# A reordered front with a third quad's scores moved into it and zero matmuls in its gaps, in a fused attention and MLP kernel

## The chip, the cores and the metric

The kernel runs on one core of a Trainium2 chip. The metric is device time in microseconds (us), the median of several executions.

The engines are named as the profile names them: PE is the matmul engine, PEld its weight load, DVE is VectorE, ACT is ScalarE, POOL is GpSimd, SP is SyncE.

## The reference

```python
# q, k, v: [8, 8, 576, 64]; f: [8, 8, 576]; w_in: [512, 2048]; w_out: [2048, 512]; all float32
scores = q @ k.T / sqrt(64)
cum    = cumsum(log(clip(f, 1e-4, 1)))
scores = where(causal, scores + cum[:, None] - cum[None, :], -1e9)
attn   = softmax(scores) @ v
x      = attn, heads side by side: [4608, 512]
out    = gelu_tanh(x @ w_in) @ w_out          # [4608, 512] float32
```

The 64 pairs of batch and head are worked on in 16 "quads" of four heads; two quads make one batch. The decay is folded into v: `vw` is v times a weight per key, so that only the exponential of the scores is needed. The MLP goes in nine chunks of 512 tokens: 64 matmuls "MLP-in", 64 matmuls "MLP-out" of 128x128 weights and 512 columns each.

## The kernel before

The program order of each engine is the order in which the code emits instructions (the schedule is manual). So a function's place in the code is its place in the queue of its engine, and an instruction that waits holds up everything behind it on that engine (in the kernel before GpSimd waits 10.74 us for v, up to 15.55, and the masks that stand behind that wait start at 16.97, though ACT had written the first exponentials by 11.8).

```python
    rounds = [(0, 512), (512, 512), (1024, 512)]        # a quad's scores, in three rounds
    # ...
    psS = ctx.enter_context(tc.tile_pool(name="psS", bufs=2, space=bass.MemoryType.PSUM))
    psO = ctx.enter_context(tc.tile_pool(name="psO", bufs=1, space=bass.MemoryType.PSUM))
    psM = ctx.enter_context(tc.tile_pool(name="psM", bufs=2, space=bass.MemoryType.PSUM))
    # ...
    def load_one(src, dst, i):
        b, h0 = i // QPB, 4 * (i % QPB)
        return nc.gpsimd.dma_start(
            out=dst[i % 2].rearrange("p a d -> p (a d)"),
            in_=src[b, h0:h0 + 4].rearrange("h (p a) d -> (h p) (a d)", p=32))
    # ... transpose_words: one VectorE transpose of k (or q) into kT (or qT)
    def make_vw(i, eng):
        h0 = 4 * (i % QPB)
        vb = v_nat[(i // QPB) % 2]
        eng.tensor_mul(
            vw[i % 2][:, 0:NT], vb[:, :, h0:h0 + 4, :],
            wT[:, i, :, :].unsqueeze(3).to_broadcast([128, NT, 4, D]))

    def copy_low(i):
        nc.vector.tensor_copy(vw[i % 2][64:128, LOW], vw[i % 2][0:64, 0])
    # ...
    def score_round(i, r, by_tile):
        off, n = rounds[r]
        tiles = [psS.tile([128, 2, 512], FP32, name="ps_s", tag="s") for _ in range(2)]
        qq, p = qT[i % 2], pt[i % 2]
        parts = []
        for (key, col, q0, nq) in pieces:
            a, z = max(col, off), min(col + nq, off + n)
            if a < z:
                parts.append((key, a - off, q0 + a - col, z - a))
        for heads in ((0, 1), (2, 3)) if by_tile else (range(4),):
            for c in range(2):
                for j, (key, c0, q0, nq) in enumerate(parts):
                    for h in heads:
                        nc.tensor.matmul(
                            tiles[h // 2][:, h % 2, c0:c0 + nq],
                            key_columns(i, key, h, c),
                            qq[32 * h:32 * h + 32, q0:q0 + nq, c],
                            start=(c == 0 and j == 0), stop=(c == 1),
                            skip_group_check=True,
                        )
        for g in range(2):
            nc.scalar.activation(p[:, 2 * g:2 * g + 2, off:off + n], tiles[g], AF.Exp, scale=scale)
    # ... mask(i, r): GpSimd affine_select on the diagonal blocks of that round
    # ... product(i, groups, spare): 24 matmuls into po (psO), or into a psS tile if spare
    def denominators(i):

        def column(h):

            return lambda t: (w_bf[:, i, t, h:h + 1] if t not in (0, LOW) else
                              w_bf[:, i, t, h:h + 1].to_broadcast([128, 32]))

        po = product(i, [(32 * h, column(h), h) for h in range(4)], False)
        den = den_pool.tile([128, S], FP32, name="den", tag="den")
        nc.vector.transpose(out=den, in_=po)
        rec = den_pool.tile([128, S // 32], FP32, name="rec", tag="rec")
        nc.vector.reciprocal(rec, den[:, 0:S:32])
        rb = den_pool.tile([128, S], FP32, name="rb", tag="rb")
        nc.vector.transpose(out=rb.rearrange("p (c j) -> p c j", j=32),
                            in_=rec.unsqueeze(2).to_broadcast([128, S // 32, 32]))
        rbs[i] = rb

    def attn_out(i, x, spare=False):
        b, u = i // QPB, i % QPB
        po = product(i, [(32 * h, lambda t, h=h: vw[i % 2][:, t, h, x:D:2], h) for h in range(4)], spare)
        nc.vector.tensor_mul(xT[:, 2 * u + x, S * b:S * (b + 1)], po, rbs[i])
    # ... mlp_in(c, pairs): 8 matmuls per pair into a psS tile, GELU on ScalarE
    # ... mlp_out(c): generator, one matmul of 64 per step; fill = mlp_out(c)
    def setup():
        nc.sync.dma_start(out=f_sb, in_=f.rearrange("b h s -> (b h) s"))
        k0 = load_qk(0)[0]
        # ... masks
        load_qk(1)
        v0 = load_v(0, 0, 4)
        after(v0[0], k0)
        v0 += load_v(0, 4, 4)
        w_in_dmas.append(load_w_in(0))
        after(w_in_dmas[0], v0[7])
        w_in_dmas.append(load_w_in(1))
        # ... memsets on VectorE, log of f, transposes of quad 0
    def step(i, j, fill, fills, extra=(None, None, None)):

        first = i is not None and i < 2
        for r in range(3):
            if i is not None:
                score_round(i, r, first)
                if i == 0 and r == 0:
                    make_w()
            if j is not None:
                if r == 0:
                    denominators(j)
                else:
                    attn_out(j, r - 1, spare=(i is None and r == 1))
            if i is not None:
                if i == 0 and r == 0:
                    transpose_k(1)
                    transpose_q(1)
                if r == 0 and first:
                    make_vw(i, nc.vector)
                    copy_low(i)
                mask(i, r)
                if r == 1 and not first:
                    make_vw(i, nc.gpsimd)
                if r == 2 and not first:
                    copy_low(i)
            if extra[r]:
                extra[r]()
            pull(fill, fills[r])
    # prepare(*quads): transpose_k, transpose_q of each, then load_qk(i + 2)
    with tc.manual_schedule():
        setup()
        step(0, None, none, (0, 0, 0),
             (None, None, lambda: w_in_dmas.extend(load_w_in(c) for c in (2, 3))))
        w_out_dmas = []
        step(1, 0, none, (0, 0, 0),
             (lambda: load_qk(2),
              lambda: w_out_dmas.extend(load_w_out(c) for c in (0, 1)),
              lambda: w_out_dmas.extend(load_w_out(c) for c in (2, 3))))
        load_qk(3)
        v1 = load_v(1)
        after(v1[0], w_out_dmas[2])
        step(None, 1, none, (0, 0, 0))
        fill = none
        for c in range(NCH):

            mlp_in(c, (0, 1))
            for x in fill:
                pass
            if c == 0:
                prepare(2, 3)
                load_v(2)
            elif c + 1 < B:
                prepare(2 * c + 3, 2 * c + 4)
                if c + 2 < B:
                    load_v(c + 2)
            for pr in range(2, NP):
                mlp_in(c, (pr,))
            fill = mlp_out(c)
            if c == 0:
                pull(fill, 6)
                step(2, None, fill, (9, 8, 7))
                prepare(4)
                step(3, 2, fill, (6, 6, 5))
                step(4, 3, fill, (5, 5, 4))
            elif c + 1 < B:
                i = 2 * c + 3
                pull(fill, 6)
                step(i, i - 1, fill, (12, 8, 8))
                step(i + 1 if i + 1 < NQ else None, i, fill, (8, 7, 7))
```

One PSUM tile `po` (`psO`, one buffer) takes the products of a quad one after another: the denominators, then two value products; each must be read by DVE before the next may start. And after the first two quads, PE fills every wait of the attention with matmuls of the MLP-out (`pull(fill, n)`); before the first MLP-in there is nothing to fill with.

The softmax here doesn't subtract the row's maximum and nothing guards it: scores larger than these inputs give would overflow.

## Time and profile before

| | before |
|---|---|
| time | 354.88 us (354.87 to 354.94) |
| span of the profiled run | 353.4 us |
| first MLP-in matmul | 32.17 us |
| first MLP-in to second MLP-in | 43.09 us |
| second to third | 35.67 us, then 36.56 each |

From the page of the profile before: the span, and the granted clock of PE in 40 slices of 8.8 us, in tenths of full rate.

```profile
span 353.4 us, 7265 instructions
...
PEclk9866999999999999999999999999999999999999
```

As far as it is recorded, the clock is low in the second to fourth slices only. The record begins at 12.34 us; that PE ran at half clock before that is read from its matmuls (a score matmul of 448 columns takes 0.56 us at 8.7, as it does at 16.2 where the record says 0.50, and 0.36 at 12.4 where it says 1.0). The windows view of before, cut at the stages; its columns are the stretch, its length, the busy time of PE, PEld, DVE, ACT and POOL (with counts), the granted clock, the share of DMA and GB/s:

```profile
0.00:32.17 32.17, 19.08 (x265) 9.57 (x267) 18.85 (x40) 16.51 (x18) 17.67 (x34) 0.80 0.92 170
32.17:46.93 14.76, 14.03 (x62) 6.27 (x63) 4.71 (x5) 7.05 (x7) 1.58 (x3) 0.98 1.18 202
46.93:75.26 28.33, 25.30 (x370) 11.43 (x373) 11.98 (x18) 19.36 (x20) 15.38 (x19) 1.00 0.75 158
75.26:110.93 35.67, 34.95 (x373) 16.04 (x379) 14.81 (x22) 22.84 (x24) 13.49 (x18) 1.00 0.42 97
```

In the front PE is busy 19 of 32 us; in the stretch of the first MLP-out 25.3 of 28.3; after that it is nearly full, 34.95 of 35.67. The PE timeline of before (start, length, engine, line, operation, out<-in, form, count, and in brackets the idle time before it with what ended it). L215 is the product with the attention weights, L255 is MLP-in:

```profile
27.64 1.53 PE L215 MATMUL po<-pt,w_bf 128*32 128x512 bf16 x24 [0.85 <-DVE xT L244]
...
30.30 1.53 PE L215 MATMUL po<-pt,vw 128*32 128x512 bf16 x24
32.17 3.73 PE L255 MATMUL ps_h<-xT,w_in_sb 128*128 128x512 bf16 x15 [0.33 <-issue]
...
62.60 0.87 PE L215 MATMUL po<-pt,vw 128*32 128x512 bf16 x24 [0.20 <-DVE den L233]
```

A product of 24 matmuls takes 1.5 us at half clock and 0.87 us at full clock. From the view of waits of before (who waited for what: total, times, longest), GpSimd stood behind a late load:

```profile
POOL w_in_sb L120 <- DMA v_nat<-in_v_dram: 10.7, 1, 10.7
```

From the chain of waits of before (start, length, what), the stretch that sets the date of the first value product of quad 2 at 62.60:

```profile
49.99 6.43 DMA v_nat<-in_v_dram
56.59 2.34 POOL vw L154
58.95 0.64 DVE vw L159
```

v of the second batch comes late, since its load waits for w_out.

### The profile page before, as it was taken

The page shows a single profiled execution, that of the slowest core. Times are in us where ns is not written, and L with a number is a line of the kernel's source. Part 1 is how long each engine was busy: PE and PEld are TensorE (multiplying, and loading weights), DVE is VectorE, ACT ScalarE, POOL GpSimd, SP SyncE. Part 2 cuts the span into 40 slices and gives each one's busy share as a digit, 9 for nine tenths or more (in the row PEclk, how much of TensorE's full clock was granted, in tenths as well). Part 3 has the DMA queues.
Part 4 walks back from the last instruction along what each step waited for, and adds up shares of the span by engine and source line. Part 5 has one row for each costly group of instructions (what it writes and reads, how often), then busy time and mean ns, then how long its engine had stood idle before and what let it go on. Part 6 is the DMA issues. An engine that isn't in the chain of part 4 may idle for free.

```text
span 353.4 us, 7265 instructions
## 1 busy us (share of the span) xinstructions
PE 327.9 (93%) x3156; PEld 150.8 (43%) x3209; DVE 128.1 (36%) x188; ACT 188.6 (53%) x188; POOL 103.9 (29%) x142
## 2 busy tenths in 40 slices
PE   1778988999999999999999999999999999999995
PEld 0334433444444444444444444444444444444442
DVE  6557024635343524352355044414530360002011
ACT  3770666675756566556664667457556633520510
POOL 4294015652154205520551055204420320000000
PEclk9866999999999999999999999999999999999999
DMA  7799999507710671059113911280110011001011
GB/s 140 154 201 192 203 231 209 100 31 167 155 40 30 145 154 63 30 117 182 55 38 87 202 42 62 63 169 32 53 40 0 32 40 51 0 32 64 25 54 66
DMA packets 50688, 33.13 MB, mean 94 GB/s; under 512 B 38816, under 2 KB 40864, under 8 KB 50656
## 3 DMA queue, kind: packets, MB, share of 16 engines
q0 software_dynamic: 7808, 13.63, 22.2%
q1 hardware_dynamic: 42848, 19.03, 20.2%
q8 instruction: 25, 0.41, 0.5%
q14 instruction: 7, 0.06, 0.0%
HBM read 36.85 MB, written 9.44 MB: 131 GB/s over the span
## 4 chain that ended last, share of the span: by engine, by line
PE 77%; DMA 8%; POOL 5%; SPq 4%; issue 2%; DVE 1%; another core or an unknown queue 1%; ACT 0%; POOLq 0%
PE ps_h L255 31%; PE pso L269 31%; PE po L215 8%; PE ps_s L179 6%; SPq L108 4%; DMA w_out_sb<-in_moe_w_out_dram 4%; DMA v_nat<-in_v_dram 3%; POOL pt L193 2%; POOL vw L154 1%; DMA k_c<-in_k_dram 1%; POOL w_in_sb L120 1%; POOL w_out_sb L124 0%; DVE kT L138 0%; DVE qT L138 0%
## 5 line engine op out<-in xcount | busy, mean ns | idle before, releaser
L269 PE MATMUL pso<-w_out_sb,gT 128*128 128x512 bf16 x534 | 128.7, 379 | 4.4 <-issue 3.3
L255 PE MATMUL ps_h<-xT,w_in_sb 128*128 128x512 bf16 x565 | 126.7, 380 | 1.6 <-ACT gT L262 0.7
L262 ACT ACTIVATE gT<-ps_h 128x1024 bf16<-128x1024 f32 x72 | 72.7, 1023 | 92.4 <-PE ps_h L255 81.7
L187 ACT ACTIVATE pt<-ps_s 128x1024 bf16<-128x1024 f32 x96 | 92.8, 1021 | 45.2 <-PE ps_s L179 32.3
L255 PEld LDWEIGHTS <-w_in_sb 128*128 128x128 bf16 x576 | 56.4, 98 | 69.3 <-issue 2.2
L193 POOL TENSOR_SCALAR_AFFINE_SELECT pt<-pt 128x512 bf16<-128x512 bf16 (+2 forms) x80 | 47.3, 600 | 113.9 <-ACT pt L187 112.6
L269 PEld LDWEIGHTS <-gT 128*128 128x128 bf16 x576 | 52.6, 98 | 62.6 <-issue 0.7
L273 DVE COPY o_st<-pso 128x512 f32<-128x512 f32 x36 | 24.8, 689 | 91.1 <-PE pso L269 87.9
L179 PE MATMUL ps_s<-qT,kT 32*128 32x64 bf16 (+3 forms) x896 | 36.2, 269 | 6.4 <-ACT pt L187 3.0
L244 DVE TENSOR_TENSOR xT<-po,rb 128x576 bf16<-128x576 f32 x30 | 22.7, 757 | 37.5 <-PE po L215 37.3
L233 DVE STREAM_TRANSPOSE den<-po 128x576 f32<-128x576 f32 x16 | 12.5, 781 | 63.2 <-PE po L215 63.2
L154 POOL TENSOR_TENSOR vw<-v_nat,wT 128x1280 bf16<-128x1280 f32 x14 | 32.6, 2327 | 0.8 <-DMA v_nat<-in_v_dram 0.8
L179 PEld LDWEIGHTS <-kT 32*128 32x128 bf16 x896 | 16.5, 94 | 31.5 <-issue 25.4
L215 PE MATMUL po<-pt,vw 128*32 128x512 bf16 (+1 forms) x720 | 27.4, 289 | 1.4 <-DVE xT L244 1.2
L129 POOL DMA_DIRECT2D k_c<-in_k_dram x16 | 9.4, 586 | 48.2 <-DVE kT L138 47.4
L138 DVE STREAM_TRANSPOSE kT<-k_c 128x576 f32<-128x576 f32 x16 | 19.9, 1247 | 9.9 <-DMA k_c<-in_k_dram 9.7
L215 PEld LDWEIGHTS <-vw 128*32 128x32 bf16 x768 | 16.3, 101 | 16.6 <-issue 9.6
L138 DVE STREAM_TRANSPOSE qT<-q_c 128x576 f32<-128x576 f32 x16 | 19.8, 1237 | 0.3 <-DMA q_c<-in_q_dram 0.3
L215 PE MATMUL po<-pt,w_bf 128*32 128x64 bf16 (+5 forms) x384 | 16.3, 295 | 2.4 <-POOL pt L193 1.4
L187 ACT ACT_TABLE_LOAD x8 | 10.3, 1283 | 6.8 <-PE ps_s L179 6.8
L237 DVE STREAM_TRANSPOSE rb<-rec 128x576 f32<-128x576 f32 x16 | 12.5, 778 | 0.5
L215 PEld LDWEIGHTS <-w_bf 128*1 128x1 bf16 (+1 forms) x384 | 7.3, 89 | 12.3 <-issue 6.3
(42 smaller groups left out, 56.7 us busy)
## 6 DMA issues: line engine op xcount, KB each, us to landing
out_dram<-o_st SPq DMA_DIRECT2D x36, 256.0 KB, 2.0
v_nat<-in_v_dram SPq DMA_DIRECT2D x28, 256.0 KB, 7.5
k_c<-in_k_dram POOLq DMA_DIRECT2D x16, 288.0 KB, 6.3
q_c<-in_q_dram POOLq DMA_DIRECT2D x16, 288.0 KB, 7.6
w_in_sb<-in_moe_w_in_dram POOLq DMA_DIRECT2D x4, 512.0 KB, 7.0
w_out_sb<-in_moe_w_out_dram POOLq DMA_DIRECT2D x4, 512.0 KB, 13.0
v_nat<-in_v_dram SPq DMA_DIRECT2D x15, 128.0 KB, 5.9
f_sb<-in_f_dram SPq DMA_DIRECT2D x1, 144.0 KB, 2.9
```

Source lines behind the costliest of these rows:

```text
L108: ins.append(nc.sync.dma_start(out=v_nat[b % 2][:n, t, h0:h0 + nh, :], in_=v[b, h0:h0 + nh, 128 * t:128 * t + n, :].rearrange("h p d -> p ...
L138: nc.vector.transpose(out=dst.rearrange("p s c -> p (s c)").bitcast(FP32) .rearrange("p (t a) -> p a t", a=S // 32), in_=src.rearrange("p ...
L154: eng.tensor_mul(vw[i % 2][:, 0:NT], vb[:, :, h0:h0 + 4, :], wT[:, i, :, :].unsqueeze(3).to_broadcast([128, NT, 4, D]))
L179: nc.tensor.matmul(tiles[h // 2][:, h % 2, c0:c0 + nq], key_columns(i, key, h, c), qq[32 * h:32 * h + 32, q0:q0 + nq, c], start=(c == 0 an ...
L187: nc.scalar.activation(p[:, 2 * g:2 * g + 2, off:off + n], tiles[g], AF.Exp, scale=scale)
L193: nc.gpsimd.affine_select(out=x, in_=x, compare_op=ALU.is_ge, fill=0.0, base=0, pattern=pattern, channel_multiplier=-1)
L215: nc.tensor.matmul(po[r0:r0 + w.shape[-1], 448 + q0:448 + q0 + nq], w, p[:, h, col:col + nq], start=(key in (0, "low")), stop=(key in ("lo ...
L244: nc.vector.tensor_mul(xT[:, 2 * u + x, S * b:S * (b + 1)], po, rbs[i])
L255: nc.tensor.matmul(ph[:, j, :], w_in_sb[:, dt, 128 * ft:128 * ft + 128], xT[:, dt, CH * c:CH * (c + 1)], start=(dt == 0), stop=(dt == N_DT ...
L262: nc.scalar.activation(gT[c % 2][:, 2 * pr:2 * pr + 2, :], ph, AF.Gelu_apprx_tanh)
L269: nc.tensor.matmul(pso, gT[c % 2][:, ft, 128 * n:128 * n + 128], w_out_sb[:, ft, :], start=(ft == 0), stop=(ft == N_FT - 1))
L273: nc.vector.tensor_copy(st, pso)
```

## The change

The intent: bring loads and work into the order in which data arrive. GpSimd shall not wait for a load ahead of other work; quad 2 is scored already in the front; zero matmuls ("fillers") are to keep PE's clock up where PE would idle; some masks become DVE multiplies by a triangle; quads 3 and 4 stay beside the first MLP-out, in a new order. The core of the diff, with cuts marked by [...]:

```diff
-    def load_one(src, dst, i):
+    def load_one(src, dst, i, a0=0, na=S // 32):
         b, h0 = i // QPB, 4 * (i % QPB)
+        s = slice(D * a0, D * (a0 + na))
         return nc.gpsimd.dma_start(
-            out=dst[i % 2].rearrange("p a d -> p (a d)"),
-            in_=src[b, h0:h0 + 4].rearrange("h (p a) d -> (h p) (a d)", p=32))
+            out=dst[i % 2].rearrange("p a d -> p (a d)")[:, s],
+            in_=src[b, h0:h0 + 4].rearrange("h (p a) d -> (h p) (a d)", p=32)[:, s])
 
     def load_qk(i):
         return [load_one(k, k_c, i), load_one(q, q_c, i)]
 
[...]
-    def score_round(i, r, by_tile):
+    idle_ps = []
+
+    def keep_busy(n, cols=512):
+
+        for _ in range(n):
+            nc.tensor.matmul(idle_ps[0][:, 0:cols], idle[:, 0:128], idle[:, 0:cols],
+                             start=True, stop=True)
+
+    def score_round(i, r, by_tile=None):
[...]
+            if by_tile and r + heads[0] > 0:
+                keep_busy(*by_tile)
[...]
+    def mask_by_product(i, r, keys=("low", 0, 1, 2, 3)):
+        p = pt[i % 2]
+        for (key, col, q0, nq) in pieces:
+            if key in keys and q0 == 128 * (0 if key == "low" else key) and \
+                    rounds[r][0] <= col < rounds[r][0] + 512:
+                m = causal[1 if key == "low" else 0]
+                nc.vector.tensor_mul(p[:, :, col:col + 128], p[:, :, col:col + 128],
+                                     m.unsqueeze(1).to_broadcast([128, 4, 128]))
 
[...]
-        k0 = load_qk(0)[0]
+        k0 = [load_one(src, dst, 0, a0, S // 64) for (src, dst) in ((k, k_c), (q, q_c))
+              for a0 in (0, S // 64)][1]
[...]
-        v0 += load_v(0, 4, 4)
-        w_in_dmas.append(load_w_in(0))
-        after(w_in_dmas[0], v0[7])
-        w_in_dmas.append(load_w_in(1))
-
+        load_v(0, 4, 4)
+        for t_ in v_nat:
+            nc.gpsimd.memset(t_[64:128, HIGH, :, :], 0.0)
+        for t_ in vw:
+            nc.gpsimd.memset(t_[0:64, LOW, :, :], 0.0)
+        nc.gpsimd.memset(w_bf[0:64, :, LOW, :], 0.0)
+
+        nc.vector.memset(idle, 0.0)
[... the memsets leave VectorE; nine zero matmuls before, twelve after the transposes of log f ...]
+        for a0 in (0, S // 64):
+            transpose_k(0, a0, S // 64)
+        for a0 in (0, S // 64):
+            transpose_q(0, a0, S // 64)
 
[... step() keeps the later quads only ...]
+    def first_quads():
+        score_round(0, 0, (1, 256))
+        make_w()
+        transpose_k(1)
+        mask(0, 0)
+        load_qk(2)
+        make_vw(0, nc.gpsimd)
+        w_in = [load_w_in(c) for c in range(2)]
+        nc.vector.tensor_copy(w_bf[:, :, 0:NT, :], wT)
+        nc.vector.tensor_copy(w_bf[64:128, :, LOW, :], wT[0:64, :, 0, :])
+        transpose_q(1)
+        for r in (1, 2):
+            score_round(0, r, (2, 384))
+            mask_by_product(0, r)
+        copy_low(0)
+        transpose_k(2)
+        transpose_q(2)
+
+        score_round(1, 0, (2, 384))
+        mask(1, 0)
+        w_in.append(load_w_in(2))
+        make_vw(1, nc.gpsimd)
+        score_round(1, 1, (2, 256))
+        denominators(0, lambda: mask_by_product(1, 1))
+        score_round(1, 2, (1, 256))
+        mask_by_product(1, 2, (2,))
+        mask(1, 2, (3,))
+        w_in.append(load_w_in(3))
+        load_qk(3)
+        attn_out(0, 0)
+        attn_out(0, 1)
+        copy_low(1)
+
+        score_round(2, 0, (1, 256))
+        denominators(1)
+        score_round(2, 1, (1, 256))
+        w_out = [load_w_out(c) for c in range(4)]
+        attn_out(1, 0)
+        attn_out(1, 1)
+        score_round(2, 2, (1, 256))
+        for r in range(3):
+            mask(2, r)
+        v1 = load_v(1, 0, 4)
+        after(v1[0], w_out[1])
+        load_v(1, 4, 4)
+        return v1
+
+    def second_quads(fill, v1):
+
+        transpose_k(3)
+        transpose_q(3)
+        for r in range(3):
+            score_round(3, r)
+            mask(3, r)
+            pull(fill, 7 - (r > 0))
+        after(load_qk(4)[0], v1[-1])
+        make_vw(2, nc.gpsimd)
+        make_vw(3, nc.gpsimd)
+        denominators(2)
+        copy_low(2)
+        pull(fill, 6)
+        attn_out(2, 0, True)
+        pull(fill, 6)
+        attn_out(2, 1)
+        transpose_k(4)
+        transpose_q(4)
+        load_qk(5)
+        pull(fill, 6)
+        for r in range(3):
+            score_round(4, r)
+            if r == 0:
+                denominators(3)
+                copy_low(3)
+            else:
+                attn_out(3, r - 1)
+            mask(4, r)
+            pull(fill, 7)
+        load_qk(6)
 
[...]
-        step(0, None, none, (0, 0, 0),
-             (None, None, lambda: w_in_dmas.extend(load_w_in(c) for c in (2, 3))))
-        w_out_dmas = []
-        step(1, 0, none, (0, 0, 0),
-             (lambda: load_qk(2),
-              lambda: w_out_dmas.extend(load_w_out(c) for c in (0, 1)),
-              lambda: w_out_dmas.extend(load_w_out(c) for c in (2, 3))))
-        load_qk(3)
-        v1 = load_v(1)
-        after(v1[0], w_out_dmas[2])
-        step(None, 1, none, (0, 0, 0))
+        v1 = first_quads()
         fill = none
         for c in range(NCH):
 
             mlp_in(c, (0, 1))
             for x in fill:
                 pass
-            if c == 0:
-                prepare(2, 3)
+            if c > 0 and c + 1 < B:
+                prepare(2 * c + 3, 2 * c + 4)
+            if c == 1:
                 load_v(2)
-            elif c + 1 < B:
-                prepare(2 * c + 3, 2 * c + 4)
-                if c + 2 < B:
-                    load_v(c + 2)
+            if c > 0 and c + 2 < B:
+                load_v(c + 2)
+            if c == 1:
+                make_vw(4, nc.gpsimd)
[...]
-                step(2, None, fill, (9, 8, 7))
-                prepare(4)
-                step(3, 2, fill, (6, 6, 5))
-                step(4, 3, fill, (5, 5, 4))
+                second_quads(fill, v1)
```

## The prediction

> **What bounds the kernel now.** The span is 353.4 us, PE busy 93% (page). From about 76 us it is a steady PE-bound loop: the chain of waits repeats every 36.57 us per MLP chunk, against 128 matmuls x 0.2156 us plus two quads of about 4.2 us = 36.0. The diff hardly touches it; the slack lies before 76 us. (a) First MLP-in matmul at 32.17 us (PE timeline), with two quads, about 8.4 us of full-clock work, done. (b) From the end of the first MLP-in (46.93) to the equivalent end of the first MLP-out (about 76.0) PE needs about 24.4 us (64 matmuls 13.8, nine score rounds 5.6, six products 5.0) and takes 29.1. There the chain goes w_out, v (landed 56.4), GpSimd's vw (2.33), DVE's copy and k/q transposes, quad 2's first product at 62.6.
>
> **Front, costed.** Removed: GpSimd's 10.7 us wait for v ahead of w_in and masks (wait view). So quad 2's k/q are issued near 13 instead of 22.8 and, at the observed 4.5 us latency and 1.5 us per load, land near 18 and 19.4. But DVE now transposes them (2.4 us) before quad 0's denominators, whose transposition starts near 20.3 (before: 20.79). From there runs the same serial chain through the single po buffer: product on PE (0.8 to 1.5), DVE pass 0.76, six times, mask multiplies and score rounds between. I get quad 1's last product near 30.6 and quad 2's last exps at 32.3 and 33.2, which free the PSUM tiles for MLP-in: start 32.3 to 33.5 us. The front is not shorter; its gain is quad 2's three rounds already scored (1.9 us of PE).
>
> **Zero matmuls.** Before, the granted clock averages 0.79, 0.67, 0.86 in the stretches 10-20, 20-30, 30-40 us. [...] The fillers (21 of 512 columns, then about 6900 columns) should warm the first scores, but ACT and DVE pace this front: under 1 us.
>
> **First MLP-out.** Quad 3's exps end about 10.8 us after MLP-in's end, as quad 2's did (46.93 to 57.7). GpSimd then does two masks (1.3), issues k4/q4 (1.1), and only then vw of quad 2 (2.33), then DVE's copy: quad 2's first product again near 62.8 to 64, a PE stall of about 4 us. Second new stall: k4/q4 transposes (2.4 us) stand on DVE behind quad 2's last multiply, with six matmuls (1.3 us) to cover: about 1.8 us. These eat the three rounds saved. End of first MLP-out: 76 before, 76 to 79 after.
>
> **Predicted: 355.0 us, 8-in-10 range 349.5 to 359.5.** Faster by over 2%: 0.14; within 2%: 0.79; slower by over 2%: 0.07. The sum is +1 to +3 us; I shade it down because the filler counts look tuned on a chip.
>
> **What would show it.** Right: MLP-in starts at 32 to 34 us; DVE's first den transposition near 20 follows a wait on q_c; a 3 to 4 us PE wait ended by vw/copy near 62 and one of about 2 us at quad 4's first scores, ended by DVE's qT; period still 36.6; clock 1.0 at 6 to 20 us.
>
> **What would make it wrong.** MLP-in starting near 28 (q2 landing by 16) would move everything 4 to 5 us earlier: near 349. Half clock through the whole product chain, or late w_in, would make it slower.

That the fillers would speed up the first scores, and "under 1 us" for it, were my estimates; measured later, the clock stood at 1.0 from 5.93 us in the change and, as read from the matmuls, at one half up to 12.34 in the kernel before.

## The result, and the profile after

The changed kernel took 371.28 us (369.77 to 372.77, four runs) against 354.91 of the kernel before (354.87 to 355.99): slower, ratio 1.0454, 95% interval 1.0404 to 1.0503. Ratios here are the mean time of one kernel's fast runs over that of the other's of the same rounds, so not quite the ratio of the medians quoted. The profiled run took 369.77.

From the page of the profile after:

```profile
span 368.1 us, 7422 instructions
...
PEclk9995899879999999999999999999999999999999
```

The windows view after, at the same stages, and then two windows of 3.41 us, the step of the recorded clock (in every trace here its changes lie a multiple of 3.41 us apart):

```profile
0.00:38.05 38.05, 33.04 (x364) 14.59 (x365) 25.19 (x48) 20.60 (x22) 23.33 (x41) 0.85 1.02 181
38.05:53.69 15.64, 14.96 (x66) 6.47 (x65) 0.53 (x1) 9.37 (x9) 1.22 (x2) 0.94 0.78 142
53.69:89.07 35.38, 26.97 (x322) 11.01 (x320) 13.84 (x17) 14.12 (x15) 11.53 (x15) 0.90 0.28 58
89.07:125.87 36.80, 35.25 (x378) 15.74 (x376) 14.96 (x21) 22.28 (x23) 15.90 (x20) 1.00 0.67 142
...
23.00:26.41 3.41, 1.56 (x37) 0.90 (x36) 2.44 (x5) 0.00 (x0) 3.41 (x6) 1.00 1.13 209
26.41:29.83 3.42, 3.42 (x44) 1.39 (x45) 1.22 (x3) 2.05 (x2) 2.92 (x5) 0.50 1.07 182
```

The span grew by 14.7 us (368.1 - 353.4). The first MLP-in starts 5.88 us later; from there to the second MLP-in it takes 51.02 us (15.64 + 35.38) instead of 43.09, which is 7.93 more; from the second to the third 36.80 instead of 35.67, 1.13 more. After that the chunks take 36.56 us in both, and the end is 0.3 us shorter. Of the 7.93 and the 1.13, 0.65 us only change place: the kernel before does the last three MLP-out matmuls after the second MLP-in has begun.

The clock stands at 1.0 from 5.93 to 26.41 us, thanks to the fillers (in x5 below, without those in the score rounds, it falls at 17.2), then at one half until 40.07, and again at one half from 70.79 to 77.61. The last two lines above are the windows on either side of the first fall: in the one up to 26.41 PE was busy 1.56 of 3.41 us.

The PE timeline after (L237 is the product, L174 a filler, L192 scores, L278 MLP-in, L292 MLP-out):

```profile
21.77 0.87 PE L237 MATMUL po<-pt,vw 128*32 128x512 bf16 x24 [0.35 <-DVE den L255]
24.85 0.87 PE L237 MATMUL po<-pt,vw 128*32 128x512 bf16 x24 [2.21 <-DVE xT L267]
...
27.57 1.53 PE L237 MATMUL po<-pt,w_bf 128*32 128x512 bf16 x24
...
34.01 1.53 PE L237 MATMUL po<-pt,vw 128*32 128x512 bf16 x24 [0.87 <-DVE xT L267]
...
38.05 4.61 PE L278 MATMUL ps_h<-xT,w_in_sb 128*128 128x512 bf16 x16
...
69.16 0.40 PE L237 MATMUL ps_o<-pt,vw 128*32 128x512 bf16 x4 [3.12 <-POOL vw L157]
71.53 1.10 PE L237 MATMUL ps_o<-pt,vw 128*32 128x64 bf16 x20 [1.97 <-DVE vw L162]
...
79.88 0.69 PE L192 MATMUL ps_s<-qT,kT 32*128 32x64 bf16 x24 [1.28 <-DVE qT L141]
```

Four idle stretches of PE stand out: 2.21 us ahead of quad 0's second value product, after which the clock falls; 3.12 and 1.97 us at quad 2's first value product; 1.28 us at quad 4's scores. What ended them is in the timelines of GpSimd and DVE. GpSimd after:

```profile
20.53 2.33 POOL L157 TENSOR_TENSOR vw<-v_nat,wT 128x1280 bf16<-128x1280 f32 x1 [0.29 <-DMA v_nat<-in_v_dram]
...
23.59 0.76 POOL L122 DMA_DIRECT2D w_in_sb<-in_moe_w_in_dram  x1
...
66.74 4.64 POOL L157 TENSOR_TENSOR vw<-v_nat,wT 128x1280 bf16<-128x1280 f32 x2
```

DVE after:

```profile
20.98 0.74 DVE L255 STREAM_TRANSPOSE den<-po 128x576 f32<-128x576 f32 x1
...
21.94 1.20 DVE L223 TENSOR_TENSOR pt<-pt,causal 128x512 bf16<-128x512 bf16 x1
...
23.76 0.38 DVE L223 TENSOR_TENSOR pt<-pt,causal 128x512 bf16<-128x512 bf16 x1
...
69.14 2.34 DVE L162 COPY vw<-vw 64x256 bf16<-64x256 bf16 x1 [2.55 <-POOL vw L157]
```

A mask multiply takes 1.20 us and, two instructions later, one of the same shape takes 0.38. The slow one runs while GpSimd multiplies vw (20.53 to 22.86) and ends at 23.14, 0.28 us after it; the quick one runs while GpSimd only issues a load of w_in. The copy takes 2.34 us and ends at 71.48; GpSimd's two vw multiplies of 66.74 to 71.38 end just before. My hypothesis from these numbers: a mask multiply or a copy on DVE that begins while GpSimd multiplies vw ends only after that multiply. The experiments test it. The order of arrival matters: quad 0's first mask multiply began at 14.56, just after a vw multiply (14.39), and took 2.44 us; in x2 and x4 below it began just before that multiply and took 0.42 and 0.43. There it cost nothing further on: the third of these multiplies ends at 17.67 here and at 17.61 and 17.75 there.

### The profile page after: what moved, and what is told of

Read it like the earlier page. It is cut to its first block, busy times and chain, and to the rows that moved or that the text cites. A ratio compares the mean times of both kernels' runs of the same rounds, so it can differ in the third digit from the quotient of the medians.

```text
span 368.1 us, 7422 instructions
## 1 busy us (share of the span) xinstructions
PE 348.6 (95%) x3252; PEld 155.3 (42%) x3252; DVE 132.3 (36%) x192; ACT 189.2 (51%) x188; POOL 107.8 (29%) x146
## 4 chain that ended last, share of the span: by engine, by line
PE 70%; SPq 3%; POOL 3%; DVE 3%; DMA 2%; issue 2%; ACT 0%; POOLq 0%
PE pso L292 31%; PE ps_h L278 26%; PE po L237 8%; PE ps_s L192 5%; SPq L110 3%; POOL vw L157 2%; DMA v_nat<-in_v_dram 2%; DVE vw L162 1%; POOL pt L206 1%; PE ps_o L237 1%; DVE o_st L296 0%; DVE kT L141 0%; DVE qT L141 0%; ACT pt L200 0%; DVE den L255 0%
## 5 line engine op out<-in xcount | busy, mean ns | idle before, releaser
L292 PE MATMUL pso<-w_out_sb,gT 128*128 128x512 bf16 x576 | 136.3, 383 | 0.0
L278 PE MATMUL ps_h<-xT,w_in_sb 128*128 128x512 bf16 x576 | 128.1, 381 | 1.4 <-ACT gT L285 1.4
L206 POOL TENSOR_SCALAR_AFFINE_SELECT pt<-pt 128x512 bf16<-128x512 bf16 (+2 forms) x75 | 44.0, 594 | 144.4 <-ACT pt L200 138.8
L278 PEld LDWEIGHTS <-w_in_sb 128*128 128x128 bf16 x576 | 56.4, 98 | 70.6 <-issue 3.7
L292 PEld LDWEIGHTS <-gT 128*128 128x128 bf16 x576 | 53.0, 98 | 63.7 <-issue 2.7
L192 PE MATMUL ps_s<-qT,kT 32*128 32x64 bf16 (+3 forms) x896 | 39.8, 267 | 3.5 <-ACT pt L200 1.9
L157 POOL TENSOR_TENSOR vw<-v_nat,wT 128x1280 bf16<-128x1280 f32 x16 | 37.2, 2330 | 9.4 <-DMA v_nat<-in_v_dram 9.4
L237 PE MATMUL po<-pt,vw 128*32 128x512 bf16 (+1 forms) x720 | 28.3, 293 | 4.4 <-DVE xT L267 3.1
L192 PEld LDWEIGHTS <-kT 32*128 32x128 bf16 x896 | 17.3, 94 | 29.7 <-issue 22.5
L237 PEld LDWEIGHTS <-vw 128*32 128x32 bf16 x768 | 16.3, 101 | 26.6 <-issue 12.6
L141 DVE STREAM_TRANSPOSE kT<-k_c 128x576 f32<-128x576 f32 (+1 forms) x17 | 19.9, 1181 | 4.3 <-DMA k_c<-in_k_dram 4.3
L141 DVE STREAM_TRANSPOSE qT<-q_c 128x576 f32<-128x576 f32 (+1 forms) x17 | 19.8, 1174 | 0.8 <-DMA q_c<-in_q_dram 0.7
L237 PE MATMUL po<-pt,w_bf 128*32 128x64 bf16 (+5 forms) x384 | 14.7, 288 | 0.1
L174 PE MATMUL idle_ps<-idle 128*128 128x512 bf16 (+2 forms) x43 | 12.8, 404 | 1.3 <-DVE idle L318 1.3
(47 smaller groups left out, 72.3 us busy)
```

What stands on the lines that cost most here:

```text
L141: nc.vector.transpose(out=dst.rearrange("p s c -> p (s c)").bitcast(FP32) .rearrange("p (t a) -> p a t", a=S // 32)[:, a0:a0 + na], in_=sr ...
L157: eng.tensor_mul(vw[i % 2][:, 0:NT], vb[:, :, h0:h0 + 4, :], wT[:, i, :, :].unsqueeze(3).to_broadcast([128, NT, 4, D]))
L174: nc.tensor.matmul(idle_ps[0][:, 0:cols], idle[:, 0:128], idle[:, 0:cols], start=True, stop=True)
L192: nc.tensor.matmul(tiles[h // 2][:, h % 2, c0:c0 + nq], key_columns(i, key, h, c), qq[32 * h:32 * h + 32, q0:q0 + nq, c], start=(c == 0 an ...
L206: nc.gpsimd.affine_select(out=x, in_=x, compare_op=ALU.is_ge, fill=0.0, base=0, pattern=pattern, channel_multiplier=-1)
L237: nc.tensor.matmul(po[r0:r0 + w.shape[-1], 448 + q0:448 + q0 + nq], w, p[:, h, col:col + nq], start=(key in (0, "low")), stop=(key in ("lo ...
```

## The experiments

Theory: the front loses because a DVE mask multiply is held up by GpSimd's vw multiply (2.21 us gap), the gap drops PE's clock, and the serial chain of products then runs at half rate up to 40 us; the first MLP-out loses because of GpSimd's order (3.12 us), a DVE copy held up in the same way (1.97 us) and a second fall of the clock. Rivals: the late arrival of v or other DMA traffic; the serial chain over one `po` buffer by itself, now longer by quad 2's scores; the fillers' own time.

| kernel | median us | ratio to before, 95% | first MLP-in | first to second | clock at half before 80 us |
|---|---|---|---|---|---|
| before | 354.9 | 1 | 32.17 | 43.09 | to 12.3; 15.8 to 22.6; 26.0 to 32.8 |
| the change | 371.3 | 1.0454 (1.0404 to 1.0503) | 38.05 | 51.02 | 26.4 to 40.1; 70.8 to 77.6 |
| x1_vw_early | 366.5 | 1.0299 (1.0238 to 1.0359) | 39.17 | 45.51 | 24.5 to 41.6; 75.7 to 79.1 |
| x2_vw3_late | 372.3 | 1.0451 (1.0409 to 1.0492) | 40.02 | 52.60 | 24.5 to 45.0; 72.3 to 79.1 |
| x3_fill_gap | 366.2 | 1.0283 (1.0240 to 1.0326) | 34.34 | 49.90 | 64.8 to 71.7 |
| x4_mask_on_gpsimd | 369.6 | 1.0379 (1.0328 to 1.0430) | 37.56 | 50.18 | 26.3 to 39.9; 70.7 to 74.1 |
| y1_both | 359.0 | 1.0105 (1.0061 to 1.0149) | 34.97 | 43.00 | none |
| x5_no_fillers | 365.4 | 1.0266 (1.0220 to 1.0311) | 36.65 | 50.02 | 17.2 to 30.9; 68.4 to 75.2 |
| b1_before_fillers | 357.4 | 1.0048 (1.0020 to 1.0077) | 34.85 | 42.69 | 20.7 to 30.9 |
| z1_best | 357.7 | 1.0061 (1.0028 to 1.0094) | 36.33 | 40.05 | 28.4 to 38.7 |
| x6_front_no_port_clash | 363.9 | 1.0233 (1.0199 to 1.0266) | see below | see below | see below |
| z2_no_port_clash | 353.2 | 0.9919 (0.9880 to 0.9958) | 34.61 | 40.32 | 30.6 to 37.4 |
| z3_no_round_fillers | 354.8 | 0.9970 (0.9935 to 1.0006) | 33.81 | 40.47 | 16.5 to 26.7; 33.6 to 37.0 |
| z4_last_gap_filled | 351.7 | 0.9867 (0.9834 to 0.9901) | 33.06 | 38.92 | none |
| x7_no_late_fillers | 365.8 | 1.0262 (1.0218 to 1.0306) | 34.00 | 49.66 | 26.5 to 29.9; 64.0 to 70.8 |

The last three columns are of the one profiled run of each; half clock is listed from the first matmuls on for before, and from 6 us on for the others. All runs gave correct results.

### x1_vw_early: the vw multiplies ahead of quad 3's masks

```diff
         transpose_q(3)
+        make_vw(2, nc.gpsimd)
+        make_vw(3, nc.gpsimd)
         for r in range(3):
             score_round(3, r)
@@
         after(load_qk(4)[0], v1[-1])
-        make_vw(2, nc.gpsimd)
-        make_vw(3, nc.gpsimd)
         denominators(2)
```

> The two vw multiplies of quads 2 and 3 stand on GpSimd ahead of quad 3's masks instead of behind them. Theory A (in the first MLP-out PE waits for GpSimd's program order, 3.12 us, then for a DVE copy[...], 1.97 us, and this idling halves the clock from 70.8 to 77.6, worth about 2.5 us): both gaps and the clock dip go, the wait for quad 4's qT (1.28 us) stays or grows to 2; stretch from first MLP-out matmul to the start of the second MLP-in falls from 35.4 to about 28 us, time about 363.5. Rival B (v's arrival or DMA traffic sets the date): vw waits for v where it now stands, stretch within 1 us of 35.4, time 370 to 372.

Measured: ratio 1.0299 instead of 1.0454, and 45.51 us from first to second MLP-in instead of 51.02, so 5.5 us came back. The vw multiplies ran at 46.64, when the part of v that they need had just landed, some 20 us sooner. GpSimd timeline of this run:

```profile
46.64 4.70 POOL L157 TENSOR_TENSOR vw<-v_nat,wT 128x1280 bf16<-128x1280 f32 x2 [4.98 <-DMA v_nat<-in_v_dram]
...
67.54 0.56 POOL L132 DMA_DIRECT2D q_c<-in_q_dram  x1
68.07 0.56 POOL L132 DMA_DIRECT2D k_c<-in_k_dram  x1
```

The gap of 3.12 us is gone, the copy is quick. DVE timeline of this run:

```profile
67.92 0.23 DVE L162 COPY vw<-vw 64x256 bf16<-64x256 bf16 x1
```

The same copy takes 0.23 us when no vw multiply runs, though GpSimd was issuing loads then. v had landed by 49.4 us in the change, 17 us before its vw multiplies, so the rival of late loads falls. A dip of the clock of 3.4 us remained in the first MLP-out, and the wait for quad 4's q grew to 1.71 us, as theory A had allowed. The time was 3 us over the number expected. In the profiled run (365.21), the stretch from the first MLP-out matmul to the second MLP-in took 29.7 us instead of 28, and the front's half clock lasted longer still, so that the first MLP-in came 1.12 us later than in the change.

### x2_vw3_late: only quad 3's vw multiply moved, behind two more loads

```diff
         make_vw(2, nc.gpsimd)
-        make_vw(3, nc.gpsimd)
@@
         load_qk(5)
+        make_vw(3, nc.gpsimd)
         pull(fill, 6)
```

> Only quad 3's vw multiply is moved, behind the issue of quad 5's loads, so that nothing runs on GpSimd while DVE copies the low block of quad 2. Theory A[...]: that copy takes 0.4 to 0.6 us instead of 2.34, the second PE gap (1.97 us) goes, the first (3.12 us) stays; 2 us less, up to 4 if the clock then does not dip: 367 to 369. Rival (a copy of 64x256 is slow there for another reason, such as landing data or its own shape): it stays at 2.3 us and the time at 370 to 372.

A miss, and an instructive one: ratio 1.0451, unchanged. The copy became slower, not quicker. DVE timeline of this run:

```profile
72.54 3.47 DVE L162 COPY vw<-vw 64x256 bf16<-64x256 bf16 x1 [2.56 <-POOL vw L157]
```

GpSimd timeline of this run, the instructions it overlaps:

```profile
72.43 0.60 POOL L132 DMA_DIRECT2D k_c<-in_k_dram  x1
73.02 0.55 POOL L132 DMA_DIRECT2D q_c<-in_q_dram  x1
73.56 2.36 POOL L157 TENSOR_TENSOR vw<-v_nat,wT 128x1280 bf16<-128x1280 f32 x1
```

The copy was ready at 72.54 and ended at 76.01, 0.1 us after the end of the vw multiply (75.92). It waited through two issues of DMAs and a multiply that only began a microsecond after it. So I had put it behind a longer row of GpSimd instructions. Why the copy did not end during the two issues stays open, since in x1 the same copy took 0.23 us beside two such issues. For the 1.97 us the reading is firm: in all nine traces in which this copy of quad 2 began while a vw multiply ran (the change, x3 to x7, z2 to z4), it took 2.34 us and ended 0.1 us after the multiply; the copies of this kind that met no vw multiply took 0.22 to 0.70.

### x3_fill_gap: eight more zero matmuls in the 2.21 us gap

```diff
         attn_out(0, 0)
+        keep_busy(8)
         attn_out(0, 1)
```

> Eight more zero matmuls of 512 columns (1.7 us at full clock) between quad 0's two value products, where PE idles 2.21 us at 22.6. Theory C ([...]half-clock products and scores on the serial chain are most of the front's loss): clock stays 1.0 past 26.4, first MLP-in near 33 us instead of 38.05, time about 365 to 366. Rival D (the serial chain over DVE through one po buffer, with three score rounds now inside it, sets the date): PE only burns waiting time, first MLP-in within 1 us of 38, time 370 to 372.

Theory C laid the fall of the clock at 26.4 to that gap. The clock stayed at 1.0 through the whole front, and the first MLP-in came at 34.34 instead of 38.05; ratio 1.0283. PE timeline of this run (one of the eight is missing from the trace):

```profile
23.36 1.67 PE L174 MATMUL idle_ps<-idle 128*128 128x512 bf16 x7 [0.16 <-issue]
...
34.34 3.61 PE L278 MATMUL ps_h<-xT,w_in_sb 128*128 128x512 bf16 x15 [0.39 <-ACT pt L200]
```

Nothing else was changed, no wait was removed, and PE did more work. So 3.7 of the 5.9 us lost in the front are the half clock (3.1 by y1 below, which has the same front at full clock and reached 34.97). The rest is not: 34.34 is still later than 32.17.

### x4_mask_on_gpsimd: the slow DVE mask back to GpSimd

```diff
-        denominators(0, lambda: mask_by_product(1, 1))
+        mask(1, 1)
+        denominators(0)
```

> The mask of quad 1's second round goes from a DVE multiply by the triangle back to GpSimd, behind its vw multiply. Theory E (the DVE multiply takes 1.20 us instead of 0.38[...], and this makes the PE gap long enough to drop the clock): quad 0's first multiply by rb starts near 23.2 instead of 24.06, PE gap 1.4 instead of 2.2; if the clock then holds to 30 us, first MLP-in near 33 and 365 us; if it falls all the same, first MLP-in near 37 and 369 to 370. Rival: no change of either.

Half of it: quad 0's first multiply by rb started at 23.68 instead of 24.06, the gap was 1.91 us, and the clock fell all the same at 26.3; first MLP-in 37.56, 369.6 us, near the second branch of the expectation. The other DVE mask multiply of quad 1 had come next, and met the same vw multiply (21.15 to 23.48) in place of the first: it took 1.07 us and ended 0.29 us after it.

### y1_both: x1 and x3 together

The edit is the sum of the two diffs above.

> The two edits that helped, together: vw multiplies of quads 2 and 3 ahead of quad 3's masks, and eight more zero matmuls between quad 0's value products. If the front's half clock and GpSimd's order in the first MLP-out are separate causes, the gains add: 5 and 5 to 6 us off, 359 to 361; first MLP-in near 34.3, second MLP-in starting near 78. If they share a cause (one clock story), the sum is smaller: 363 to 366. Either way above the kernel before, as 34.3 is later than its 32.17 and the qT wait of 1.7 us remains.

Ratio 1.0105. The gains add: 0.0155 from x1, 0.0171 from x3, 0.0349 together. In the profiled run the clock never fell. What is left of the loss there, 3.7 us of span, lies 2.8 us in the front (34.97 against 32.17) and 1.25 in the second MLP-out (36.92 against 35.67), with 0.3 us less at the end. So the two stages have separate causes, and the front's half clock and GpSimd's order with the held-up copy in the MLP-out account for about three quarters of the loss (0.0349 of 0.0454).

### x5_no_fillers and b1_before_fillers: the fillers alone

x5 leaves out the fillers inside the score rounds of the changed kernel:

```diff
-        for _ in range(n):
+        for _ in range(n if cols == 512 else 0):
             nc.tensor.matmul(idle_ps[0][:, 0:cols], ...)
```

> The zero matmuls inside the score rounds are left out, the 21 before the first scores stay. Theory F (they hold the clock up to 26 us, and their own cost is nothing while it is up): clock falls near 16 to 20 us, first products and scores at half rate, first MLP-in 39 to 41 us, time 371 to 374. Rival G (ACT and DVE pace the front, and after 26 us the fillers only cost time at half clock, about 0.2 us each): first MLP-in 37 to 38, time 368 to 371.

I was wrong here, and so was the rival in its size: without the fillers the changed kernel is faster, 1.0266 against 1.0454. The clock fell at 17.2, as theory F said, but it was back at 30.9, before the last products and the MLP-in. With the fillers it fell 9 us later and came back 9 us later. My reading is that half clock on quad 0 and 1's scores costs little, since ACT paces those (its exponentials take 0.97 us per tile back to back), and costs more on the last products and the MLP-in; no run separates this. The profiled run shows only part of the gain: it is the slowest of its four, 2.4 us faster than the profiled run of the change, where the medians differ by 5.9.

b1 puts fillers into the kernel before and changes nothing else in its order:

```diff
+            if by_tile and i + r + heads[0] > 0:
+                keep_busy(2, 384 if i == 0 else 256)
@@ setup
+        keep_busy(9)          # ... and keep_busy(12) behind the transposes of log f
@@ step
+                    if j == 1 and i is None:
+                        keep_busy(3)
                     denominators(j)
+                    if j == 0 and r == 2:
+                        keep_busy(4)
                     attn_out(j, r - 1, ...)
```

> The kernel before with zero matmuls alone: 21 of 512 columns before the first scores, two per half round of quads 0 and 1, four before quad 0's second value product, three before quad 1's denominators; order of all else untouched. If the idea of filling gaps is sound and its order of work was what lost: clock 1.0 from about 6 us on, first MLP-in near 30.5 instead of 32.17, time 352 to 354. If fillers delay the products or do not hold the clock: 355 to 357.

The second branch of the expectation, and a little worse: ratio 1.0048, slightly slower, first MLP-in 34.85 instead of 32.17. The clock fell at 20.66, after quad 0's denominators had waited for masks, and stayed low for three windows. In the first of these windows PE was recorded as busy throughout. Windows view of this run:

```profile
20.66:24.07 3.41, 3.41 (x32) 1.07 (x36) 3.31 (x4) 1.45 (x2) 3.16 (x6) 0.50 1.10 207
```

A busy PE at half clock was not enough to bring the clock back. Nor was there much to win: of the kernel before's own runs, the ten with a mean clock of 0.995 or more took 354.9 to 357.2 us (mean 355.6), the nineteen with 0.984 or less 354.6 to 358.1 (mean 356.1). So in this order of work the half clock cost little, half a us in the means, and in the change's 3.1 to 3.7 us (x3, y1).

### x7_no_late_fillers: without quad 2's fillers only

```diff
-        score_round(2, 0, (1, 256))
+        score_round(2, 0, (0, 256))       # the same for rounds 1 and 2
```

> The changed kernel without the fillers of quad 2's score rounds only (six matmuls of 256 columns); halves of the heads stay in their order. Hypothesis H ([...]the clock stayed at half for four windows of 3.41 us although PE is recorded 95% busy): the clock still falls near 26 but is back after one or two windows, at 30 to 33, first MLP-in near 35.5, ratio about 1.03. Rival I (the fillers cost only their own 1.5 to 2 us at half clock): clock low until about 40 as before, first MLP-in 36.3 to 37, ratio 1.038 to 1.042.

Six matmuls of 256 columns fewer, and the first MLP-in comes at 34.00 instead of 38.05; ratio 1.0262. The clock fell at 26.45, after the same gap, and was back at 29.86, after one window instead of four. PE timeline of this run:

```profile
25.75 1.04 PE L192 MATMUL ps_s<-qT,kT 32*128 32x64 bf16 x24
26.73 1.53 PE L237 MATMUL po<-pt,w_bf 128*32 128x512 bf16 x24
...
31.40 0.87 PE L237 MATMUL po<-pt,vw 128*32 128x512 bf16 x24 [0.87 <-DVE xT L267]
```

Windows view of this run, the window in which the clock came back:

```profile
26.45:29.86 3.41, 3.41 (x50) 1.27 (x48) 2.10 (x5) 2.54 (x3) 3.15 (x5) 0.50 1.12 208
```

PE is recorded busy 3.41 of 3.41 us in this window, as in the changed kernel's at 26.41, yet one was followed by full clock and the other by half. What differs is the work: here the score matmuls of a round run in one group (24, then 16), in the change in two halves (12 and 12, 8 and 8) with a filler of zeros between. The unprofiled runs agree: the mean clock is 0.981 to 0.991 in x7's four runs, 0.963 to 0.972 in the change's. So in this front the fillers, once the clock had fallen, kept it down: at half for 13.66 us in the change, with PE recorded busy 12.79 of them, and for 3.41 us in x7. Hypothesis H had the fillers between the half rounds keep the clock down, as they did; how they do it, by being zeros or by dividing the rounds, these runs do not separate; it is left open.

### x6_front_no_port_clash: the clash with GpSimd's vw multiply taken out of the front

```diff
-        make_vw(1, nc.gpsimd)             # behind load_w_in(2)
@@
-        mask_by_product(1, 2, (2,))
-        mask(1, 2, (3,))
+        mask(1, 2, (2, 3))
         w_in.append(load_w_in(3))
         load_qk(3)
+        make_vw(1, nc.gpsimd)
@@
-        copy_low(1)                       # now behind denominators(1)
```

> The changed kernel with one thing moved in its front: quad 1's vw multiply on GpSimd stands behind the issue of w_in and k3/q3 (its DVE copy behind quad 1's denominators), and quad 1's last mask is GpSimd's alone[...]. No filler is added. Theory[...]: the DVE mask near 22 us takes 0.38 instead of 1.20, the 2.21 us PE gap shrinks to about 1.3, the clock holds past 26.4, first MLP-in near 34, first MLP-out unchanged; ratio to before about 1.03 instead of 1.045. Rival (the serial chain alone leaves PE idle enough): the clock still falls near 26 and first MLP-in stays at 37 or later, ratio 1.04 or more.

Ratio of the fast runs 1.0233. The three timed runs took 363.77 to 363.94 with a mean clock of 0.991; the profiled one took 369.24 with 0.972 and counts as slow. In its trace the mask multiply takes 0.36 us, as expected. DVE timeline of this run:

```profile
22.04 0.36 DVE L223 TENSOR_TENSOR pt<-pt,causal 128x512 bf16<-128x512 bf16 x1
```

and the PE gap is 1.25 us instead of 2.21. Of that difference about 0.84 us is the clash (1.20 - 0.36); the edit also takes the second mask multiply (0.30 us of the chain) off DVE. But in that run the clock fell at 23.63, and the first MLP-in came at 38.40. A mean clock of 0.991 over 362 us means about 6.5 us at half rate, two windows of 3.41, where the profiled run has six before 80 us (17.1 us in the front, 3.4 in the first MLP-out); so the three fast runs lost at most two windows in the front, and if their dip in the first MLP-out is as long as in the change, none. That is worked out from the mean, since those runs left no trace. GpSimd's vw multiply beside it is thus shown as the cause of the slow mask (0.36 us without, 1.20 with); that the slow mask alone decides whether the clock falls is not shown, as one run of four fell without it.

### z1_best, z2_no_port_clash, z3_no_round_fillers, z4_last_gap_filled: the repaired kernel

z1 takes out each cost in turn:

```diff
@@ first_quads
-        transpose_q(2)
@@
-        make_vw(1, nc.gpsimd)
@@
-        mask_by_product(1, 2, (2,))
         mask(1, 2, (3,))
         w_in.append(load_w_in(3))
         load_qk(3)
+        make_vw(1, nc.gpsimd)
         attn_out(0, 0)
+        transpose_q(2)
+        keep_busy(4)
         attn_out(0, 1)
-        copy_low(1)
+        mask_by_product(1, 2, (2,))
@@
         denominators(1)
+        copy_low(1)
@@ second_quads
         transpose_q(3)
+        make_vw(2, nc.gpsimd)
+        make_vw(3, nc.gpsimd)
+        after(load_qk(4)[0], v1[-1])
+        load_qk(5)
+        copy_low(2)
+        copy_low(3)
         for r in range(3):
             score_round(3, r)
             mask(3, r)
-            pull(fill, 7 - (r > 0))
-        after(load_qk(4)[0], v1[-1])
-        make_vw(2, nc.gpsimd)
-        make_vw(3, nc.gpsimd)
+            pull(fill, (11, 8, 2)[r])
+        transpose_k(4)
         denominators(2)
-        copy_low(2)
+        transpose_q(4)
         pull(fill, 6)
         attn_out(2, 0, True)
-        pull(fill, 6)
+        pull(fill, 4)
         attn_out(2, 1)
-        transpose_k(4)
-        transpose_q(4)
-        load_qk(5)
@@
-                copy_low(3)
```

> The changed kernel with every cost that the runs showed taken out: fillers in the value-product gap; quad 1's vw multiply on GpSimd behind the issue of w_in and k3/q3[...]; quad 2's q transposed and quad 1's last DVE mask done after quad 0's multiplies; vw multiplies, their DVE copies and the loads of quads 4 and 5 ahead of quad 3's masks; quad 4 transposed beside quad 2's denominators; more MLP-out matmuls between quad 3's first rounds. First MLP-in near 33, first MLP-out 26 to 27 us long instead of 35.4, second MLP-in near 74.5 (before: 75.3), time 353 to 355, equal to the kernel before or 1 us better. If the reordering itself, not those side costs, is the loss, it stays above 358.

Ratio 1.0061: above the expectation, though the first MLP-out did as hoped (40.05 us from first to second MLP-in, less than the 43.09 of before). The front did not: I had walked into the same trap. DVE timeline of this run:

```profile
24.27 3.10 DVE L223 TENSOR_TENSOR pt<-pt,causal 128x512 bf16<-128x512 bf16 x1
```

GpSimd timeline of this run:

```profile
24.73 2.34 POOL L157 TENSOR_TENSOR vw<-v_nat,wT 128x1280 bf16<-128x1280 f32 x1
```

The mask multiply, moved to where GpSimd issues loads (22.91 to 24.71) and then multiplies vw, took 3.10 us and ended at 27.37, 0.30 after GpSimd's multiply. An issue of w_in did not hold such a multiply up (0.38 us at 23.76 in the change), so why this one had not finished by 24.73 is open. PE waited 1.53 us and the clock fell at 28.41.

z2 gives that mask to GpSimd, and loads v of the third batch directly behind the second's:

```diff
-        mask(1, 2, (3,))
+        mask(1, 2, (2, 3))
-        mask_by_product(1, 2, (2,))
@@
         load_v(1, 4, 4)
+        load_v(2)
@@ chunk 1
-            if c == 1:
-                load_v(2)
```

> The repaired kernel of the last call, where quad 1's DVE mask took 3.10 us[...]: that mask goes to GpSimd, and v of the third batch is loaded right behind the second's. The 1.53 us PE gap at 25.9 and the half clock from 28.4 to 38.6 go: first MLP-in near 32.5 instead of 36.3, second MLP-in 40 us later at 72.5 (before: 75.3), the 0.8 us wait for vw in the second MLP-out goes: time 351 to 353, ratio about 0.99. If the clock falls all the same: 355 to 357.

Ratio 0.9919, 95% interval 0.9880 to 0.9958: a little faster than the kernel before. The runs fell into two groups, 351.3 to 352.0 with a mean clock of 1.00, and 354.4 to 354.5 with 0.988. In the profiled run, of the second group, PE had idled 0.87 us between quad 1's value products and the clock had fallen at 30.6. The wait in the second MLP-out is gone, 35.68 us from second to third MLP-in instead of 36.80 in the change.

z3 is z2 without any filler after the first scores:

```diff
-        for _ in range(n):
+        for _ in range(n if cols == 512 else 0):
@@
-        keep_busy(4)
+        keep_busy(4, 508)                 # so left out too
```

> The same without any zero matmul after the first scores. If fillers only shift the half-clock stretch and cost time, as leaving them out of the changed kernel suggested (5 us faster): as fast as with them or faster, 350 to 352. If in a chain without long gaps they do hold the clock through quad 1's products: clock falls near 17 us and is back near 31, products take 1.5 instead of 0.87 us, first MLP-in 1.5 to 2.5 us later, time 353 to 355.

Ratio 0.9970 (0.9935 to 1.0006), 352.8 to 355.9: in between, and not clearly different from either. Whether the fillers of z2 help is thus not shown; those of z4 below do, all its runs being under 352.1 and all of z3's over 352.7 (the intervals of the ratios are apart too). They were run at other times.

z4 is z2 with three more fillers where PE still idled:

```diff
         attn_out(1, 0)
+        keep_busy(3)
         attn_out(1, 1)
```

> The repaired kernel that beat the kernel before (ratio 0.992), with three more zero matmuls between quad 1's two value products, where PE still idled 0.87 us. Its runs came in two groups, 351.3 to 352.0 with a mean clock of 1.00 and 354.4 to 354.5 with 0.988; if the last idle gap decides which, all runs now fall in the first group: 351 to 352, ratio 0.988. If the clock still falls in some runs, the two groups stay. If the fillers delay the chain, the fast group moves up by 0.5 us.

Ratio 0.9867 (0.9834 to 0.9901), 1.3% faster: 351.69 us, six runs within 351.52 to 352.06, all with a clock of 0.999 or 1.0. One group is left. Windows view of this run at the stages:

```profile
0.00:33.06 33.06, 29.96 (x370) 13.59 (x373) 23.14 (x46) 20.44 (x23) 23.82 (x42) 1.00 1.00 181
33.06:47.71 14.65, 13.86 (x63) 6.24 (x65) 1.28 (x2) 9.20 (x9) 1.65 (x3) 1.00 1.18 210
47.71:71.98 24.27, 22.82 (x316) 10.31 (x321) 13.19 (x17) 14.12 (x15) 11.18 (x15) 1.00 0.67 135
```

Compared with the kernel before, the first MLP-in is still 0.9 us later, but the stretch to the second takes 38.92 us instead of 43.09. That is what the idea was worth in this repaired form, once its side costs were gone; I put it down to quad 2's scores out of the first MLP-out and v there in time, which no run separates.

## Why the prediction was wrong

The prediction was 355.0 us with a range of 349.5 to 359.5 and 0.79 on "within 2%"; measured 371.28. It looked at the right two stages, and two steps failed. In the front it costed the product chain at full clock, with at most 1.3 us lost; the clock was halved there and 5.88 us were lost. In the first MLP-out it had one wait of about 4 us and took the saved scores to pay for it, so 0 to 3 us lost; there were two waits, 3.12 and 1.97 us, and a second fall of the clock, and from the first MLP-in to the second it took 7.93 us more.

- "MLP-in: start 32.3 to 33.5 us." Failed: 38.05. The failed term is, for the larger part, the clock. The prediction said of the zero matmuls "under 1 us" and costed the chain at full clock; it named "half clock through the whole product chain" as what would make it slower, and that happened: x3 shows 3.7 us of it by filling one gap, x7 4.0 us by leaving out six fillers. Quad 1's last product came at 34.01 instead of 30.6. The prediction costed no part of its front at half clock; but already in the kernel before the clock fell, at 15.76 and 26.00, after windows in which PE was busy 1.96 of 3.42 us, and here it fell after one of 1.56 of 3.41 us, which held most of the gap of 2.21 us.
- "DVE pass 0.76, six times, mask multiplies and score rounds between", with no word of what GpSimd does meanwhile. Failed: a mask multiply takes 0.36 us with nothing on GpSimd (x6) and 1.20 us against its vw multiply. I did not check the moved multiplies against what would run on GpSimd at that time.
- "DVE's first den transposition near 20 follows a wait on q_c": right, 20.98, behind a wait of 0.41 us for q. "The front is not shorter": right, and with full clock (x3) it was 34.34.
- "A PE stall of about 4 us" at quad 2's first product, for GpSimd's order: right in kind. It was 3.12 us for GpSimd's order and another 1.97 us for the DVE copy that ended 0.1 us after the second vw multiply, which the prediction did not have; 5.5 us came back in x1. It missed also the second fall of the clock (70.8 to 77.6), which came after a window with PE busy 0.40 of 3.41 us.
- "About 1.8 us" at quad 4's scores: 1.28 in this run, 1.71 in x1 and others. Right in kind, and in size in those.
- "End of first MLP-out: 76 before, 76 to 79 after": failed, 89.07, as the sum of the above.
- "The diff hardly touches" the loop from 76 us on: nearly. The second MLP-out waited 0.81 us for vw, since v of the third batch was loaded late, and 0.68 us at its MLP-in, where the kernel before has three matmuls left to fill. From 126 us on the period is 36.56 in both.

What stays open: why fillers between the half rounds keep the clock down once it has fallen, and what makes it fall. The share of time that PE is recorded busy in a window does not decide it alone: over these traces the clock fell after windows with PE busy from 11% (x3, 61.41 to 64.83) to 77% (z3, 13.07 to 16.48), and held after windows of 49% (x1, 58.63 to 62.04) and 54% (the change, 57.13 to 60.55). Open too are the two cases in which DVE waited through issues of k and q (x2, z1).

## What to carry to other kernels

Before moving work between DVE and GpSimd, list what the other engine runs at that moment: here a DVE mask multiply or copy that began while GpSimd multiplied vw ended only after that multiply (0.28 and 0.1 us after it in the change), so a 0.2 us copy cost 2.3 us, and once, begun ahead of two DMA issues and a vw multiply, 3.5 (x2). Zero matmuls paid here where they covered the long idle gaps, so that the clock never fell (the profiled runs of y1 and z4: 1.0); put in between the score rounds alone (the change against x5) they only moved the half-clock stretch to a later and dearer place (from 17.2 to 30.9 us to 26.4 to 40.1, with 5.9 us between the medians). Two groups of times with two mean clocks, as in z2, were the sign of one gap, of 0.87 us, with which the clock sometimes fell; filling it made the kernel both faster and steady (z4, 351.5 to 352.1).
